# The second parity's value stores go from ScalarE's DMA queue to SyncE's

## The chip, the cores and the metric

One core of a Trainium2 chip runs the kernel. The metric is the device time of one execution in microseconds (us); before the change the median of three runs is 625.64 us. TensorE (PE) multiplies, VectorE (DVE) and ScalarE (ACT) copy, add and evaluate functions, GpSimd (POOL) issues accumulating transfers, and SyncE (SP) does nothing but issue transfers (DMAs). ScalarE can issue transfers too, and the change is about that. An engine runs its instructions in order: one that waits holds up all that stand behind it on that engine, computing ones included.

## The reference

For 2048 tokens x of width 512 the program computes g·a + (1 − g)·b, where g is a sigmoid gate of each token, a is attention with 32 heads of width 16 in which each token looks at itself and at 7 earlier tokens at distances 2, 4, ... 14, and b is a gated feed-forward net of width 1792.

```
q, k, v = split(x @ wqkv)                       # 32 heads of 16
idx = pos[:, None] - arange(8)[None, :] * 2     # 8 tokens, 2 apart
attn = softmax(where(idx >= 0, q . k[idx] * 16**-0.5, -1e9))
a = (sum over the 8 of attn * v[idx]) @ wo
b = (gelu(x @ w_gate) * (x @ w_up)) @ w_down
out = g * a + (1 - g) * b,   g = sigmoid(sum(x * gate_w))
```

## The kernel before, in words

**Parities.** The distances are even, so even and odd tokens never meet in the attention. The kernel does the even tokens first (`par` 0), then the odd ones (`par` 1), each as 8 tiles of 128 tokens, `jj` 0 to 7. The two halves run through the same stages: projections, then 14 feed-forward steps `f`.

**Projections.** `project` and `project_one` go through a parity's 8 tiles for a block `cb` of the weights `wqkv`: block 0 makes keys and queries of the first 16 heads, block 1 the values of both halves of the heads with the gate's column, block 2 keys and queries of the other 16 heads. Each product (L189, tile `acc` or `p` in PSUM) is made from numbers split in two parts, high and low, so it takes three matmuls for each of four slices of 128. Block 1 has two PSUM tiles for each `jj`, 16 in all, which take the four banks `acc0` to `acc3` in turn: a bank can be filled again only after its last tile was copied out.

**Taking a tile out.** `take` does that. ScalarE copies the PSUM tile into a staging tile in SBUF (L211; `hh` and `hl` in turn, six buffers of each; the last three of block 2 use `c`), a transfer stores it to memory in HBM (L215, `vs` for values, `ks` for keys; for keys there is a second one at L217 for the queries, `qs`), and for every other value tile ScalarE copies the gate's column (L219, tile `z`). A staging buffer can be written again only after the transfers that read it have landed. The attention reads `ks`, `qs`, `vs` back later, shifted by token: tiles `kq` (L270, L271, L267) and `v` (L270, L271).

**Around the values of the second parity.** At the same time SP loads what comes next: the weights of block 2 (`r`, L173, which ScalarE at L162 and VectorE at L87 split into `d`), feed-forward weights (`raw`, L461 and L463; `r`, L415; `g` from `ws`, L435), and the attention's `kq`. POOL adds into `g` (L440). VectorE runs the attention of the first parity (L286 to L337) and of the feed-forward (L488 to L495) in between.

**What sets the order.** The code is written as one stream; a scheduler that simulates a time line puts the instructions of each engine in order and adds the semaphore waits. Where one engine's queue changes, it may put other instructions in another order too. Transfers from SP and ACT share eight semaphores, `DMAHW0` to `DMAHW7`, which are given out in turn over both queues. A transfer waits, before it is issued, until the last transfer with its semaphore has landed, whichever engine issued that one. So ScalarE can be held by a store, and SP by a load of its own eight transfers ago.

**Which queue.** One line of `take` chooses (L214). Before, it sends keys and queries of the first parity and of the second head half to SP, and the rest to ACT: the second parity's keys and queries of block 0 (16 transfers), and all values (16 transfers in each parity).

Of the kernel before, what the change touches and what calls it, by code (L numbers as in the profile page):

```python
# [44 lines left out]
def tile_gated_mix(ctx: ExitStack, tc: tile.TileContext, xt, wqkv, wff, wo, out):  # L45
    nc = tc.nc
# [10 lines left out]
    def tl(tag, dt=F32):  # L57
        return pool.tile([P, COLS.get(tag, 512)], dt, name=tag, bufs=BUFS[tag])
# [146 lines left out]
    def rows(t, jj):  # L205
        return t.rearrange("c (p j) d -> j p c d", j=NP)[jj]

    def take(ps, par, jj, hh, vals, tag=None):
        st = tl(tag or next(stages))[:, :512]
        n = CU if vals else 512  # L210
        nc.scalar.activation(st[:, :n], ps[:, :n], AF.Copy)  # L211
        two = st.rearrange("p (a c d) -> p a c d", a=2, c=2)
        dst = VS[par, hh] if vals else KS[par, hh]
        queue = nc.sync if not vals and (hh or not par) else nc.scalar  # L214
        queue.dma_start(rows(dst[:, W:], jj), two[:, 0])  # L215
        if not vals:
            queue.dma_start(rows(QS[par, hh], jj), two[:, 1])  # L217
        elif not hh:
            nc.scalar.activation(z[:, par, jj:jj + 1], ps[:, CU:CU + 1], AF.Copy)  # L219

    def project(par, cb, bg=iter(())):
        for jj in range(NP):
            if cb == 1:
                for hh in range(2):

                    ps = bank(f"acc{(2 * jj + hh) % BT}")
                    qkv_mm(ps, par, jj, 1, range(KC), (CU, 0)[hh], (WQ, CU)[hh])
                    take(ps, par, jj, hh, True)
            else:
                ps = bank(next(names))  # L230
                qkv_mm(ps, par, jj, 0, range(KC))
                take(ps, par, jj, 0, False)
            next(bg, None)
            pull((2.7, 2.2)[par])
        done.add((par, cb))
        if cb == 1:
            en = pool.tile([P, 64], F32, name="en")[:, :NP]
            nc.scalar.activation(en, z[:, par], AF.Exp, scale=-1.0)
            nc.vector.tensor_scalar_add(en, en, 1.0)
            nc.vector.reciprocal(g[:, par], en)  # L240
            nc.vector.tensor_scalar(gc[:, par], g[:, par], -1.0, 1.0, op0=OP.mult, op1=OP.add)

    def project_one(par, jj):

        ps = bank(f"acc{jj % BT}")
        qkv_mm(ps, par, jj, 2, range(KC))
        take(ps, par, jj, 1, False, tag=None if jj < 5 else "c")
        pull((2.7, 2.2)[par])
        if jj == NP - 1:
            done.add((par, 2))  # L250
# [640 lines left out]
```

## Time and profile before

| what | value |
|---|---|
| median of three runs | 625.64 us (623.52 to 625.9) |
| the profiled execution, its own time | 623.92 us |
| its span in the trace | 622.1 us |
| TensorE busy | 606.0 us (97%) |
| TensorE weight loads | 505.5 us (81%) |
| VectorE busy | 514.1 us (83%) |
| ScalarE busy | 378.3 us (61%) |
| transfers issued by SP (q1) | 92.69 MB |
| transfers issued by ACT (q10) | 6.43 MB |

The span is the trace's own length, from which places in time are counted; the execution's time is 1.8 us longer. "Busy" leaves out the time in which an engine issues transfers or waits. In the chain of waits each piece is followed back to what released it; a row of the timeline gives start, length, engine, line and operation, and in brackets the idle time ahead of it with what ended that. `ACTq` and `SPq` are the instruction queues of ScalarE and SP: their DMA rows are issues, not the transfers. The second parity's values are made in the stretch from about 317 us to 344 us of the span.

### The profile page before, as it was taken

The numbers are of one execution on the slowest core, as the hardware profiler recorded it, in microseconds if no ns is written. First come the engines' busy times: TensorE is split into PE (matmuls) and PEld (weight loads), VectorE is DVE, ScalarE is ACT, GpSimd is POOL, SyncE is SP. The second block draws the span as 40 slices with busy tenths as digits, with TensorE's granted clock in tenths as the row PEclk, the third lists the DMA queues.
The fourth block names the chain that finished last, engine by engine and source line by source line (L and its number), as shares of the span: only waits on it lengthen the run. The fifth ranks groups of instructions, "written<-read, shape, count | busy, mean of one in ns | idle before, by whom it ended". The sixth has DMA issues, their size and how long they took to land.

```text
span 622.1 us, 8227 instructions
## 1 busy us (share of the span) xinstructions
PE 606.0 (97%) x2839; PEld 505.5 (81%) x2839; DVE 514.1 (83%) x598; ACT 378.3 (61%) x634; POOL 82.5 (13%) x110
## 2 busy tenths in 40 slices
PE   8999999999999999999996999999999999999997
PEld 7898877877888888888896887888888887888886
DVE  6949698969979797845985997999898979898881
ACT  6654456765776877764482337566766585685732
POOL 0141021111111111101100001111111011101200
PEclk9999999999999999999997999999999999999999
DMA  8399959796899988985478948886878597937624
GB/s 272 122 252 249 340 142 301 185 283 196 240 240 237 306 211 241 253 244 190 136 214 264 268 144 212 257 232 153 251 184 241 135 259 185 272 97 196 94 58 160
DMA packets 85591, 132.48 MB, mean 213 GB/s; under 512 B 8111, under 2 KB 52271, under 8 KB 85550
## 3 DMA queue, kind: packets, MB, share of 16 engines
q1 hardware_dynamic: 59678, 92.69, 45.2%
q0 software_dynamic: 12672, 32.84, 28.1%
q10 hardware_dynamic: 13200, 6.43, 3.5%
q8 instruction: 22, 0.36, 0.2%
q14 instruction: 19, 0.16, 0.1%
HBM read 67.18 MB, written 36.77 MB: 167 GB/s over the span
## 4 chain that ended last, share of the span: by engine, by line
PE 71%; DMA 13%; issue 7%; DVE 6%; ACT 2%; SPq 0%; POOL 0%; ACTq 0%; POOLq 0%; DVEq 0%
PE p L478 32%; PE acc L518 10%; PE acc L189 10%; PE p L518 10%; PE p L740 5%; DMA g<-raw 4%; DMA raw<-wff 4%; PE acc L740 2%; DMA vs<-hh 2%; PE p L189 2%; DMA c<-wqkv 1%; DMA d<-r 1%; DMA raw<-xt 1%; DVE prod L324 1%; DVE prod L286 1%
## 5 line engine op out<-in xcount | busy, mean ns | idle before, releaser
L478 PE MATMUL p<-S,g 128*128 128x512 f32 x672 | 166.4, 389 | 0.5 <-DVE c L488 0.5
L478 PEld LDWEIGHTS p<-S,g 128*128 128x128 f32 x672 | 126.0, 188 | 27.0 <-DVE c L488 0.9
L478 PE MATMUL p<-A,g 128*128 128x512 f32 x504 | 128.1, 391 | 3.9 <-DMA g<-raw 1.6
L478 PEld LDWEIGHTS p<-A,g 128*128 128x128 f32 x504 | 93.8, 188 | 26.3 <-DMA g<-raw 3.6
L286 DVE TENSOR_TENSOR prod<-kq 128x2048 f32<-128x2048 f32 x32 | 73.0, 2282 | 14.6 <-DMA kq<-kq 5.8
L440 POOL DMA_DIRECT2D g<-raw x42 | 36.4, 874 | 329.4 <-ACT g L439 202.5
L324 DVE TENSOR_TENSOR prod<-v,lg 128x2048 f32<-128x2048 f32 x32 | 73.0, 2280 | 6.3 <-DMA v<-vs 4.8
L289 DVE TENSOR_REDUCE lg<-prod 128x128 f32<-128x2048 f32 x32 | 73.0, 2282 | 0.3
L518 PE MATMUL p<-d,hh 128*128 128x512 f32 x224 | 68.7, 389 | 0.0
L518 PE MATMUL acc<-d,hh 128*128 128x512 f32 x224 | 60.5, 390 | 1.1 <-DMA d<-r 1.1
L444 ACT ACTIVATE g<-raw 128x1024 fp32r<-128x1024 f32 (+1 forms) x42 | 41.3, 988 | 18.8 <-PE p L478 18.8
L518 PEld LDWEIGHTS acc<-d,hh 128*128 128x128 f32 x224 | 42.0, 188 | 10.7 <-DMA d<-r 1.9
L518 PEld LDWEIGHTS p<-d,hh 128*128 128x128 f32 x224 | 42.0, 188 | 8.8
L439 ACT ACTIVATE g<-raw 128x1024 fp32r<-128x1024 f32 (+1 forms) x42 | 41.3, 983 | 10.5 <-DVE raw L421 9.7
L488 DVE TENSOR_TENSOR c<-p,s 128x512 f32<-128x512 f32 x56 | 38.1, 684 | 11.3 <-PE p L478 11.0
L492 DVE TENSOR_TENSOR c<-c 128x512 f32<-128x512 f32 x56 | 38.3, 685 | 10.7 <-ACT c L584 10.2
L483 ACT ACTIVATE s<-p 128x512 f32<-128x512 f32 x56 | 33.1, 593 | 17.3 <-PE p L478 17.1
L495 DVE TENSOR_TENSOR hl<-c,hh 128x512 fp32r<-128x512 f32 x56 | 38.2, 683 | 6.2 <-ACT hh L494 6.2
L518 PE MATMUL p<-d,hl 128*128 128x512 f32 x112 | 42.9, 389 | 0.0
L494 ACT ACTIVATE hh<-c 128x512 fp32r<-128x512 f32 x56 | 35.0, 625 | 11.6 <-DVE c L492 11.2
L531 ACT ACTIVATE rt<-p 128x512 f32<-128x512 f32 x48 | 28.0, 595 | 20.2 <-PE p L518 20.0
L328 DVE TENSOR_TENSOR prod<-prod 128x1024 f32<-128x1024 f32 x32 | 39.0, 1219 | 0.3
(145 smaller groups left out, 915.1 us busy)
## 6 DMA issues: line engine op xcount, KB each, us to landing
g<-raw POOLq DMA_DIRECT2D x28, 512.0 KB, 6.6
raw<-wff SPq DMA_DIRECT2D x42, 256.0 KB, 4.0
ws<-g SPq DMA_DIRECT2D x14, 768.0 KB, 6.1
g<-ws SPq DMA_DIRECT2D x14, 768.0 KB, 5.9
r<-wff SPq DMA_DIRECT2D x28, 256.0 KB, 4.4
d<-r POOLq DMA_DIRECT2D x28, 256.0 KB, 6.6
g<-raw POOLq DMA_DIRECT2D x14, 384.0 KB, 6.0
v<-vs SPq DMA_DIRECT2D x8, 512.0 KB, 7.4
```

Of the source, the lines that this page charges most:

```text
L189: LAST[:] = [nc.tensor.matmul(ps[:, :cn], a[:, t], w[:, c0:c0 + cn], start=(kc == 0 and n == 0), stop=(kc == KC - 1 and n == 2))]
L286: paced(nc.vector.tensor_tensor(prod, spans(k, jj), q[:, jj:jj + 2, None, :].to_broadcast([P, 2, W, UC]), op=OP.mult))
L289: nc.vector.tensor_reduce(two_of(lg, jj), prod.rearrange("p j w (h d) -> p (j w) h d", d=DH), axis=AX.X, op=OP.add)
L324: paced(nc.vector.tensor_tensor(prod.rearrange("p j w (h d) -> p (j w) h d", d=DH), spans(v, jj).rearrange("p j w (h d) -> p j w h d", d=D ...
L328: nc.vector.tensor_tensor(prod[:, :, :4], prod[:, :, :4], prod[:, :, 4:], op=OP.add)
L439: nc.scalar.activation(lo, raw, AF.Copy, scale=-1.0)
L444: ins = nc.scalar.activation(hi, raw, AF.Copy)
L478: LAST[:] = [nc.tensor.matmul(ps, w_, a_, start=(start and kc == 0 and n == 0), stop=(kc == 1 and n == 2), skip_group_check=True)]
L492: nc.vector.tensor_tensor(ge, ge, up, op=OP.mult)
L495: nc.vector.tensor_tensor(hl_, ge, hh_.bitcast(F32), op=OP.subtract)
L518: LAST[:] = [nc.tensor.matmul(pp, a[:, ts], w, start=(i == 0 and n == 0 and gr == 0), stop=(i == 1 and n == 2), skip_group_check=True)]
L740: LAST[:] = [nc.tensor.matmul(pa, a, b, start=(first and n == 0), stop=(last and n == 2), skip_group_check=True)]
```

## The change

One condition is written anew. Values of the second parity go to SP; every other store keeps its queue (keys and queries of the second parity's block 0 stay on ScalarE, as do the first parity's values).

```
-        queue = nc.sync if not vals and (hh or not par) else nc.scalar
+        queue = nc.sync if (vals if par else not vals) or hh and not vals else nc.scalar
```

So 16 transfers of 128 KB, with the waits that belong to them, leave ScalarE's stream and enter SP's. The scheduler's order is the same in both programs up to that place and differs behind it on all engines. Three places follow; in the names, numbers tell buffers apart, and in brackets stand the semaphores that an instruction waits for.

First, ScalarE's stream in the middle of the second parity's values. `hl_3188`, `hh_3168`, `hh_3205`, `hl_3224` are staging tiles, `vs10` and `vs11` the values in HBM, `d_3041` and `d_3046` the last two quarters of block 2's weights. Before:

```order
L215 DMA vs11_122<-hh_3125 128x2x128 [waits DMAHW4_49,Activation_49]
L553 ACTIVATE p_3374<-p_3367 128x512
L211 ACTIVATE hh_3168<-acc1_3155 128x256 [waits PE_49]
L215 DMA vs10_119<-hl_3151 128x2x128 [waits DMAHW6_49,Activation_49]
L211 ACTIVATE hh_3205<-acc3_3192 128x256 [waits PE_49]
L215 DMA vs10_119<-hl_3188 128x2x128 [waits DMAHW2_49,Activation_49]
L162 ACTIVATE d_3041<-r_3042 128x512 [waits DMAHW5_49]
L483 ACTIVATE s_3423<-p_3416 128x512 [waits DMASW7_49,PE_49]
L215 DMA vs11_122<-hh_3168 128x2x128 [waits DMAHW4_49,Activation_49]
L215 DMA vs11_122<-hh_3205 128x2x128 [waits Activation_49]
L211 ACTIVATE hl_3224<-acc0_3211 128x256 [waits PE_49]
L219 ACTIVATE z_132<-acc0_3211 128x1
```

and with the change:

```order
L439 ACTIVATE g1_3128<-raw_3053 128x1024 [waits DMAHW5_49,DMAHW4_49]
L444 ACTIVATE g1_3128<-raw_3053 128x1024
L211 ACTIVATE hl_3188<-acc2_3175 128x256 [waits DMAHW2_49,PE_49]
L219 ACTIVATE z_132<-acc2_3175 128x1
L483 ACTIVATE s_3423<-p_3416 128x512 [waits DMASW7_49,PE_49]
L211 ACTIVATE hh_3168<-acc1_3155 128x256 [waits PE_49]
L162 ACTIVATE d_3041<-r_3042 128x512 [waits DMAHW4_49]
L162 ACTIVATE d_3046<-r_3047 128x512 [waits DMAHW5_49,DMASW1_49]
L211 ACTIVATE hh_3205<-acc3_3192 128x256 [waits PE_49]
L211 ACTIVATE hl_3224<-acc0_3211 128x256 [waits PE_49]
L219 ACTIVATE z_132<-acc0_3211 128x1
```

The stores and their waits are gone. The two weight copies of L162 now stand together, ahead of the copy into `hh_3205`, and `L439`/`L444` stand later than before.

Second, SP's stream at the same place, from the last weights of block 2 on. Before:

```order
L461 DMA raw_3056<-ws11_748 128x512 [waits DMAHW2_49,DVE_49]
L463 DMA raw_3056<-wff 128x2x256 [waits DMAHW3_49]
L173 DMA r_3042<-wqkv 128x512 [waits DMAHW5_49,DVE_49]
L173 DMA r_3047<-wqkv 128x512 [waits DMAHW7_49,DVE_49]
L270 DMA kq_3320<-ks10_118 128x896 [waits DMAHW6_49,DMAHW1_49,DMAHW0_49]
L271 DMA kq_3320<-ks10_118 128x1024 [waits DMAHW1_49]
L267 DMA kq_3320<-qs10_120 128x1024 [waits DMAHW4_49,DMAHW3_49]
L461 DMA raw_3364<-ws21_950 128x512 [waits DMAHW6_49,DMASW2_49,Activation_49]
```

and with the change:

```order
L461 DMA raw_3056<-ws11_748 128x512 [waits DMAHW2_49,DVE_49]
L463 DMA raw_3056<-wff 128x2x256 [waits DMAHW3_49]
L173 DMA r_3042<-wqkv 128x512 [waits DMAHW4_49,DVE_49]
L173 DMA r_3047<-wqkv 128x512 [waits DMAHW5_49,DVE_49]
L215 DMA vs11_122<-hh_3125 128x2x128 [waits DMAHW6_49,Activation_49]
L215 DMA vs10_119<-hl_3151 128x2x128 [waits DMAHW7_49,Activation_49]
L270 DMA kq_3320<-ks10_118 128x896 [waits DMAHW0_49]
L215 DMA vs10_119<-hl_3188 128x2x128 [waits DMAHW1_49,Activation_49]
L271 DMA kq_3320<-ks10_118 128x1024 [waits DMAHW2_49]
L215 DMA vs11_122<-hh_3168 128x2x128 [waits DMAHW3_49,Activation_49]
L267 DMA kq_3320<-qs10_120 128x1024 [waits DMAHW4_49]
L215 DMA vs11_122<-hh_3205 128x2x128 [waits DMAHW5_49,Activation_49]
```

Stores now stand between the loads, and a load behind a store also waits until ScalarE has made the copy that this store sends.

Third, SP's stream just ahead of that, with the first value stores (`hl_3072`, `hl_3108`, `hh_3089`), with the change; before, the three `L215` rows are not there:

```order
L215 DMA vs10_119<-hl_3072 128x2x128 [waits DMAHW2_49,Activation_49]
L461 DMA raw_3053<-ws01_746 128x512 [waits DMAHW4_49,DVE_49]
L463 DMA raw_3053<-wff 128x2x256 [waits DMAHW5_49]
L215 DMA vs10_119<-hl_3108 128x2x128 [waits DMAHW7_49,Activation_49]
L215 DMA vs11_122<-hh_3089 128x2x128 [waits DMAHW1_49,Activation_49]
L461 DMA raw_3056<-ws11_748 128x512 [waits DMAHW2_49,DVE_49]
```

The load of `raw_3056` has the same semaphore as the store of `hl_3072`, five rows ahead, so it now waits for that store to land, and the weights `r_3042` and `r_3047` stand behind it.

## The prediction

> **What bounds the kernel now.** I read the page first, then the stretches of the projections, then the chain, the waits and the timelines of the worst stretch. Page:
>
> ```profile
> span 622.1 us, 8227 instructions
> ...
> PE 606.0 (97%) x2839; PEld 505.5 (81%) x2839; DVE 514.1 (83%) x598; ACT 378.3 (61%) x634; POOL 82.5 (13%) x110
> ```
>
> TensorE sets the time: 606.0 of 622.1 us. A change of queue can win only the 16.1 us in which it is idle and what its clock loses. Where these are, the stretches say (length; busy time and instructions of PE, weight loads, DVE, ACT, POOL; granted clock; DMA share; GB/s):
>
> ```profile
> 284.00:325.00 41.00, 41.00 (x229) 35.84 (x228) 33.02 (x47) 24.62 (x47) 5.26 (x9) 1.00 0.60 187
> 325.00:335.00 10.00, 5.62 (x47) 5.42 (x46) 5.44 (x6) 2.53 (x8) 0.00 (x0) 0.93 0.85 253
> 335.00:349.00 14.00, 13.20 (x72) 12.29 (x73) 11.33 (x15) 5.59 (x16) 0.87 (x1) 0.81 0.90 261
> 349.00:374.00 25.00, 25.00 (x112) 20.71 (x111) 23.86 (x17) 8.84 (x13) 0.00 (x0) 1.00 0.65 189
> 374.00:390.00 16.00, 14.91 (x67) 12.00 (x66) 12.46 (x16) 13.09 (x20) 2.59 (x3) 1.00 0.88 226
> 410.00:565.00 155.00, 154.32 (x681) 127.35 (x680) 141.84 (x148) 104.66 (x167) 17.50 (x21) 1.00 0.76 204
> ```
>
> The second and third stretch are the second parity's values: PE loses 4.4 and 0.8 us there, and of these stretches only there the clock falls (0.93, 0.81). Before and behind it PE is full or lacks about 1 us. In the chain (start, us, what):
>
> ```profile
> 323.62 10.67 DMA vs<-hh
> ...
> 335.58 0.17 ACT z L219
> 335.75 0.04 issue
> 335.80 13.53 PE acc L189 x72
> ```
>
> A store of 128 KB (`vs<-hh`) takes 10.67 us to land; ScalarE cannot issue the next store before that. Behind the issue stand the copies that empty the banks, and TensorE starts again 0.05 us after the gate's column is out. This is the program's order: the store of `hh_3168` waits for `DMAHW4`, which the store of `hh_3125` had. The waits there give the size:
>
> ```profile
> ACT hl L211 <- issue: 7.8, 1, 7.8
> DVE d L87 <- ACT d L162: 6.3, 1, 6.3
> ...
> PE acc L189 <- ACT z L219: 5.2, 1, 5.2
> ```
>
> One wait, 7.8 us on ScalarE, 6.3 on VectorE, 5.2 on TensorE.
>
> **What the change removes.** First, that wait. Second, the slow clock behind it, from TensorE's timeline:
>
> ```profile
> 326.14 0.88 PE L189 MATMUL acc<-g,rt 128*128 128x258 f32 x6
> ...
> 327.10 0.88 PE L189 MATMUL acc<-g,rt 128*128 128x256 f32 x6
> ...
> 329.03 0.88 PE L189 MATMUL acc<-g,rt 128*128 128x256 f32 x6
> ...
> 335.80 1.66 PE L189 MATMUL acc<-g,rt 128*128 128x258 f32 x6 [5.18 <-ACT z L219]
> ...
> 340.81 0.88 PE L189 MATMUL acc<-g,rt 128*128 128x258 f32 x6
> ...
> 342.26 0.88 PE L189 MATMUL acc<-g,rt 128*128 128x256 f32 x6
> ```
>
> (The first three rows serve further down.) Twelve matmuls, one tile, take 342.26 − 340.81 = 1.45 us at the full clock. The two tiles from 335.80 to 340.81 took 5.01 where 2.90 would do: 2.1 us lost. Stall and slow clock: 5.2 + 2.1 = **7.3 us**.
>
> Third, the issues themselves, and what the stores take to land:
>
> ```profile
> L215 ACTq DMA_DIRECT2D vs<-hl x8: 366/390/1058, 317.1 to 342.9; - x8
> L215 ACTq DMA_DIRECT2D vs<-hh x8: 366/366/482, 319.4 to 344.9; - x8
> DMA to landing us min/median/max: 1.8/4.1/10.7
> ```
>
> Sixteen at about 0.38 us are 6.1 us of ScalarE's stream. Without the wait they would be covered: ScalarE is busy 24.6 of 41 us in the stretch ahead. I count them as nothing; they enter through ScalarE's pace below.
>
> **What it adds on SP.** The same 6.1 us of issues, on a queue with room. It must not hold a load that somebody needs soon:
>
> ```profile
> 289.45 0.61 SPq L170 DMA_DIRECT2D c<-wqkv  x1
> 316.54 0.33 SPq L461 DMA_DIRECT2D raw<-ws  x1
> ...
> 320.14 0.33 SPq L461 DMA_DIRECT2D raw<-ws  x1
> ...
> 321.07 1.10 SPq L173 DMA_DIRECT2D r<-wqkv  x2
> 322.51 0.33 SPq L270 DMA_DIRECT2D kq<-ks  x1
> ...
> 334.74 0.32 SPq L461 DMA_DIRECT2D raw<-ws  x1
> ```
>
> SP issues nothing between 289.45 and 316.54. The urgent loads are the two `r<-wqkv`: ScalarE copies them (L162) now just ahead of the copy into `hh_3205`. In front of them come three value stores. The store of `hl_3072` goes out about 316.1 us, when its copy is done (315.65 + 0.37, below), and lands, at the median of 4.1, by 320.2; `raw_3056`, which waits for it, was issued at 320.14 anyway. So the `r` loads go out 0 to 0.5 us later than at 321.07 to 321.8. The rows of tile `r` in that stretch have landings of
>
> ```profile
> DMA to landing us min/median/max: 4.4/4.6/5.2
> ```
>
> so they are there by 325.5 to 327.5. The `kq` loads come about one store's landing later, 4.1 us (they stand behind the store of `hh_3125`), but VectorE starts on that `kq` only when the first parity's mixing is over; its timeline still has
>
> ```profile
> 344.69 2.25 DVE L324 TENSOR_TENSOR prod<-v,lg 128x2048 f32<-128x2048 f32 x1
> ```
>
> so even 7 us earlier there is room. `raw_3364` was held to 334.74 by the same kind of wait.
>
> **ScalarE's new pace.** Starting at `hh_3125` (now 319.78, some 0.4 earlier without the issue ahead of it, so 319.4), from its own rows: copy 0.39, L553 0.60, two issues for `ks` and `qs` 0.9, hl and z 0.53, table 1.28 and exp 0.63, L439 and L444 2.1, hl and z 0.52, L483 0.60 put the copy into `hh_3168` at about 327.0 and its end at 327.4. Rows are read start to start, so they overlap by some 0.1 us each and the sum is a little long. Quoted for the large ones:
>
> ```profile
> 315.65 0.37 ACT L211 ACTIVATE hl<-acc 128x256 f32<-128x256 f32 x1
> ...
> 319.78 0.39 ACT L211 ACTIVATE hh<-acc 128x256 f32<-128x256 f32 x1 [0.46 <-ACT hh L211]
> ...
> 322.26 1.28 ACT L304 ACT_TABLE_LOAD   x1
> ...
> 324.09 1.04 ACT L444 ACTIVATE g<-raw 128x1024 fp32r<-128x1024 f32 x1
> ...
> 326.39 0.65 ACT L162 ACTIVATE d<-r 128x512 fp32r<-128x512 f32 x1
> ```
>
> Then two L162 (1.2) and `hh_3205` by 329.0. TensorE wants those banks, by its rows above, at 326.1 (after `hl_3188` and its z, out at 326.3), 327.1 (after `hh_3168`, 327.4) and 329.0 (after `hh_3205`, 329.0). So it waits 0.2 to 0.5 us if the `r` loads land by 327.5, and as much more as they are late. Ends: nothing, and about 2 us if both come 2 us late. I take **0.8 us**, near the low end, since the landings vary by 0.8 only. In the stretch from 374 to 390 PE lacks 1.09 us and the clock stays at 1.00, so nothing is added for a slow clock.
>
> **Staging buffers.** A buffer comes back after twelve tiles, at 1.45 us each 17 us. The slowest of these stores took 10.67. So no copy waits for a buffer, with 6 us to spare; this cover goes if SP holds a store that long.
>
> **Behind it.** From 349 to 565 TensorE is full, so a gain made at 335 stays, if VectorE (141.84 of 155) keeps up. It loses the same gap, 6.3 us, so it falls back by 1 us at most. The scheduler's new order there I price at 0, ±1.5 us: the only gap is 16.0 − 14.91 = 1.1 us.
>
> **Sum.** 7.3 − 0.8 = 6.5 us. The profiled execution's 623.92 gives 617.4. It lies 1.7 us under the runs' median of 625.64 and near their lowest; I move up by half of that and predict **618.2 us**.
>
> **The rivals.** What speaks against the change is in the Trainium skill, "DMA: Bandwidth & Descriptors", section "Queues, rings and completion order": each DMA engine takes turns between the queue rows, packet by packet. By that, a store on ACT's row passes SP's loads and one on SP's row stands behind them. The trace disagrees for this store: on its own row it took 10.67 us while SP's loads ran. By the rule the sum would lose part of its gain in SP's row, which is rival A, at 621.5.
>
> A. *Late loads or stores, in part.* In SP's row three `kq` loads stand among the stores. If the `r` loads land at 330 to 331, or a store costs its buffer's 6 us of cover, TensorE waits 3 to 4 us in place of 0.8, with up to 1 us for the clock. For it: ScalarE now reaches L162 within 1 us of the expected landing. Against: 4.4 to 5.2 is a narrow spread. Net gain 2.3 to 4.3; 623.92 − 3.3, moved up by the same 0.8, is about 621.5.
>
> B. *The same wait in another place.* The change moves 2 MB but removes none, and the transfers' share is 0.85 to 0.90 there. If transfers and not the order of issues are the bound, ScalarE waits as long for `r` or for buffers. Against: TensorE, not transfers, was full again at 349 with 0.65. Then 624 to 625.
>
> C. *Slower.* The store of `hl_3072` is itself slow: every load behind `raw_3056` waits for it. Over all value and key stores the issue-to-landing times are
>
> ```profile
> DMA to landing us min/median/max: 1.8/3.9/12.9
> ```
>
> With 12.9, it lands at 329.0, the `r` loads go out at 330.5, land at 335.7, and the bank is free at 337.0 in place of 329.0: a gap of 8.0 us, and 2.1 for the clock, where 7.3 went: 623.92 + 2.8 = 626.7, more with another late bank. It decides if the `r` loads land after about 333. Against: SP's row is empty when that store goes out.
>
> D. *The change does nothing.* The order shows the sixteen stores gone from ScalarE; only the eight tiles of keys and queries of block 0 stay there. It can be left out.
>
> **Chances.** The forecast 0.62, its own range 615 to 621 (6.5 + 1.1 + 1 below the profiled time, and the lower gain on the median). A 0.17, B 0.13, C 0.08. Half a per cent, 3.1 us, is about what a measurement of this kernel can tell: faster means under 622.5, slower over 628.8. Faster: the forecast and most of A, 0.76; within: B, the rest of A and half of C, 0.18; slower: the other half, and a little for the new order, 0.06. The range, 614.5 to 623.5, holds the forecast and A and leaves out B and C, 2 in 10.
>
> **What would show it.** In the changed profile: no wait of ScalarE on an issue at L215 near 327; the stretch from 325 to 349 with PE full at a clock of 1.00; no 5 us on "PE acc <- ACT z"; VectorE's wait at L87 under 1 us. Against it: a wait "ACT d L162 <- DMA r" of several us (A or C), "ACT L211 <- DMA vs" (buffers), or gaps of TensorE of more than 2 us behind 349.

## The result, and the profile after

| | before | after |
|---|---|---|
| median time | 625.77 us (623.52 to 626.91, 4 runs) | 616.54 us (614.47 to 616.72, 4 runs) |
| profiled execution, its own time | 623.92 us | 614.47 us |
| its span | 622.1 us | 612.5 us |

The ratio after to before is 0.9849, 95% interval 0.9815 to 0.9884: faster by 1.5%. Predicted were 618.2 us, range 614.5 to 623.5.

The page of the changed kernel:

```profile
span 612.5 us, 8244 instructions
...
PE 602.3 (98%) x2839; PEld 503.6 (82%) x2839; DVE 514.1 (84%) x598; ACT 376.4 (61%) x633; POOL 82.5 (13%) x110
```

The same 2839 matmuls take 3.7 us less busy time and stand in a span that is 9.6 us shorter. To see where, I cut both traces at two places that both programs have: the first feed-forward matmuls among the second parity's values (`p<-A,g`), and the first matmul of block 2 (`acc<-d,A`). Between them lies the same work: 156 matmuls start there, and the rows count those at the edges too, 158 here and up to 159 further down. The stretch between the two (length; busy time and instructions of PE, weight loads, DVE, ACT, POOL; granted clock; DMA share; GB/s), before:

```profile
316.18:343.69 27.51, 22.33 (x158) 21.61 (x157) 17.41 (x24) 14.00 (x36) 0.88 (x1) 0.88 0.88 256
```

and after:

```profile
316.40:336.46 20.06, 20.06 (x158) 19.55 (x157) 18.46 (x25) 14.20 (x38) 0.89 (x1) 1.00 1.00 302
```

That is 7.45 us: 27.51 − 22.33 = 5.18 us in which TensorE stood, and 22.33 − 20.06 = 2.27 us of slow clock. Behind the second cut to the end of the span, before needs 622.1 − 343.69 = 278.41 us and after 612.5 − 336.46 = 276.04: another 2.37 us. Ahead of the first cut after is 0.22 us later. 7.45 + 2.37 − 0.22 = 9.60, the whole difference of the spans.

The chain of waits of the changed kernel, start, length and what:

```profile
320.82 1.39 PE p L478 x6
322.21 19.89 PE acc L189 x144
342.09 1.36 PE p L478 x6
```

Where the chain went through a store (`vs<-hh`, 10.67 us) and ScalarE before, there now is nothing but TensorE. ScalarE's timeline at the place of the old wait:

```profile
325.51 0.40 ACT L211 ACTIVATE hh<-acc 128x256 f32<-128x256 f32 x1
326.36 1.32 ACT L162 ACTIVATE d<-r 128x512 fp32r<-128x512 f32 x2 [0.46 <-DMA r<-wqkv]
327.58 0.37 ACT L211 ACTIVATE hh<-acc 128x256 f32<-128x256 f32 x1
...
328.86 0.39 ACT L211 ACTIVATE hh<-acc 128x256 f32<-128x256 f32 x1 [0.57 <-PE acc L189]
```

The copies into `hh_3168` (325.51) and `hh_3205` (327.58) have the two weight copies of L162 between them. The one wait left there is 0.46 us for a load. At 328.86 ScalarE waits for TensorE, and TensorE has no wait in the whole stretch. SP's timeline:

```profile
321.53 0.89 SPq L173 DMA_DIRECT2D r<-wqkv  x2
322.51 0.38 SPq L215 DMA_DIRECT2D vs<-hh  x1
...
323.46 0.74 SPq L270 DMA_DIRECT2D kq<-ks  x1
...
327.48 1.26 SPq L267 DMA_DIRECT2D kq<-qs  x1
```

The last `kq` load goes out at 327.48, 3.1 us later than before. The value stores stand between, and some are held themselves (issues of up to 1.26 us). On SP no copy stands behind them.

### The profile page after: what moved, and what is told of

Its sections match the earlier page's. It is cut to its first block, busy times and chain, and to the rows that moved or that the text cites. A ratio compares the mean times of both kernels' runs of the same rounds, so it can differ in the third digit from the quotient of the medians.

```text
span 612.5 us, 8244 instructions
## 1 busy us (share of the span) xinstructions
PE 602.3 (98%) x2839; PEld 503.6 (82%) x2839; DVE 514.1 (84%) x598; ACT 376.4 (61%) x633; POOL 82.5 (13%) x110
## 4 chain that ended last, share of the span: by engine, by line
PE 84%; DMA 6%; issue 5%; DVE 2%; ACT 1%; SPq 0%; POOL 0%; DVEq 0%; ACTq 0%; POOLq 0%
PE p L478 38%; PE acc L189 13%; PE acc L518 11%; PE p L518 11%; PE p L740 5%; PE p L189 3%; PE acc L740 2%; DMA v<-vs 1%; DMA raw<-wff 1%; DMA c<-wqkv 1%; DMA d<-r 1%; DMA raw<-xt 1%; DVE prod L324 1%; DMA ws<-raw 1%; ACT s L526 1%
## 5 line engine op out<-in xcount | busy, mean ns | idle before, releaser
L444 ACT ACTIVATE g<-raw 128x1024 fp32r<-128x1024 f32 (+1 forms) x42 | 41.3, 988 | 13.1 <-PE p L478 12.8
L439 ACT ACTIVATE g<-raw 128x1024 fp32r<-128x1024 f32 (+1 forms) x42 | 41.3, 983 | 10.3 <-DVE raw L421 10.0
```

Of the source, the lines that this page charges most:

```text
L439: nc.scalar.activation(lo, raw, AF.Copy, scale=-1.0)
L444: ins = nc.scalar.activation(hi, raw, AF.Copy)
```

## The experiments

What I held for the cause: a store that ScalarE may not issue until another transfer, the last one with the same semaphore, has landed; that other one is slow beside SP's `kq` loads; and the copies that free TensorE's banks stand behind the store that waits. The rivals: that sixteen issues were simply too much for ScalarE; that a store is late wherever it goes; that the scheduler's new order, not the stores, made the gain; and that SP's order of loads decides. Each kernel is compared with runs of the kernel before on its own chip (medians 625.81 and 625.80 us). All are cut at the same two places, as above; the last four columns are of the one profiled execution of each:

| kernel | median, us | ratio, 95% interval | to first cut | between cuts | behind | span |
|---|---|---|---|---|---|---|
| before | 625.8 | 1 | 316.18 | 27.51 | 278.41 | 622.1 |
| changed | 616.54 | 0.9849 [0.9815, 0.9884] | 316.40 | 20.06 | 276.04 | 612.5 |
| middle stores on SP | 618.73 | 0.9899 [0.9867, 0.9931] | 318.12 | 22.80 | 275.98 | 616.9 |
| the others on SP | 614.72 | 0.984 [0.9796, 0.9883] | 316.37 | 20.54 | 275.59 | 612.5 |
| all sixteen on POOL | 615.38 | 0.9851 [0.9808, 0.9893] | 317.99 | 20.06 | 276.75 | 614.8 |
| `kq` loads later only | 618.15 | 0.9886 [0.9836, 0.9936] | 318.24 | 20.06 | 279.20 | 617.5 |
| two small stores more | 626.34 | 1.0017 [0.999, 1.0043] | 316.87 | 28.98 | 278.65 | 624.5 |
| every store on SP | 621.62 | 0.9932 [0.9896, 0.9968] | 317.38 | 20.06 | 281.86 | 619.3 |
| changed, `kq` later | 615.64 | 0.9834 [0.9798, 0.987] | 316.58 | 20.07 | 276.25 | 612.9 |
| changed, again | 616.22 | 0.9848 [0.9818, 0.9879] | 317.02 | 20.07 | 276.11 | 613.2 |

The way to the first cut varies by some 2 us, and between two executions of the changed kernel by 0.6; the two columns behind it are what an edit is read from.

### The middle stores alone

Only the value stores of three tiles (`jj` 1 to 3, both halves, six stores; the store that waited before is one of them) go to SP.

```
-        queue = nc.sync if not vals and (hh or not par) else nc.scalar
+        queue = nc.sync if not vals and (hh or not par) or (vals and par and 0 < jj < 4) else nc.scalar
```

> Six of the sixteen second-parity value stores go to SP (tiles jj 1 to 3, the ones around the wait of 7.8 us); the other ten stay on ScalarE. Theory (one wait of ScalarE, at the store of hh_3168, that held for a landing): the six are enough; no issue of ScalarE waits more than 2 us between 318 and 345 us, the 5.2 us gap of TensorE and its slow clock are gone, and the span falls by 6.5 to 9.5 us, to about 613 to 616. Rival R (the gain is ScalarE's relief from sixteen issues of 0.38 us): 6/16 of the 9.6 us, so about 618.5. Rival S (later stores on ScalarE wait in its place, behind the kq loads): a gap of 3 us or more comes back a few tiles later, span 618 to 622.

Measured: 22.80 us between the cuts. The span, 616.9 us, is above what the theory gave and below both rivals, but the way to the first cut is 1.9 us longer here than before, so the span alone tells none of them apart.

```profile
318.12:340.92 22.80, 21.28 (x160) 20.10 (x159) 18.59 (x25) 12.92 (x34) 0.88 (x1) 1.00 0.94 282
```

It holds two matmuls more than the changed kernel's, feed-forward ones that the scheduler put here (six take 1.39 us in the chain above, so two 0.46). So 22.80 − 20.06 − 0.46 = 2.3 us of the 7.45 are still lost. ScalarE's and TensorE's waits from 316 to 350:

```profile
ACT d L162 <- DMA r<-wqkv: 3.6, 2, 2.5
...
ACT hl L211 <- DMA vs<-hh: 3.2, 2, 2.6
...
PE acc L189 <- ACT z L219: 1.4, 1, 1.4
```

The long wait is gone, and two smaller kinds come in its place. The stores that stayed on ScalarE wait for a store (2.6 us); in the chain of waits that is one on SP's queue, which took 6.52 us. And the `r` loads come late: in this order they stand behind the first `kq` load, ahead of which SP issued nothing for 4 us:

```profile
324.24 0.32 SPq L270 DMA_DIRECT2D kq<-ks  x1
...
325.13 0.86 SPq L173 DMA_DIRECT2D r<-wqkv  x2
```

So the order of SP's loads can cost something, as a rival said, and a store on SP can hold one on ScalarE. TensorE's 1.4 us end with the second wait; how the 2.3 us divide between the loads and the stores that stayed, the trace doesn't separate.

### The other ten, with the middle six left on ScalarE

```
+        queue = nc.sync if not vals and (hh or not par) or (vals and par and not 0 < jj < 4) else nc.scalar
```

> The reverse: the ten other value stores of the second parity go to SP, the six of tiles jj 1 to 3 stay on ScalarE. Theory: stores that stand beside the loads of kq are still on ScalarE, so one of them (hh_3168 or hh_3205) still holds ScalarE for a landing of 5 to 11 us; TensorE has a gap of 2 to 6 us near 328 to 336 and the span is 617 to 622. Rival R: 10/16 of the gain, about 616, without a gap of more than 1 us.

Measured: I had expected a wait of 5 to 11 us to remain, since the store that waited is still on ScalarE, and a span of 617 to 622. No such wait remained, and the span is 612.5; the rival with its 10/16 of the gain missed too. The stretch:

```profile
316.37:336.91 20.54, 20.54 (x161) 19.94 (x160) 19.15 (x26) 14.06 (x38) 0.89 (x1) 1.00 0.98 293
```

TensorE never stands. The 0.48 us above 20.06 are two feed-forward matmuls again. Yet the four stores issued from 324 to 329, three of them on ScalarE, are as slow as before:

```profile
DMA to landing us min/median/max: 7.0/9.4/10.4
```

So a slow store alone does no harm, and it isn't the place of this store that makes the wait. What differs is who holds its semaphore: in this order the store of `hh_3168` follows the store of `hl_3151`, which went out at 321.62, ahead of the first `kq` load at 323.21, and landed within 3.1 us.

### All sixteen on POOL's queue

```
+        queue = nc.gpsimd if vals and par else nc.sync if not vals and (hh or not par) else nc.scalar
```

> All sixteen go to GpSimd's queue. Theory: that they leave ScalarE is what counts, whatever takes them; the gap of 5.2 us is gone and the span is 612.5 to 617. Rival Q (SP's row is the better one, since there the stores stand in line with the loads): on a third row the stores take 10 us and more beside the loads; but as nobody waits for them on ScalarE, a loss could come through staging buffers alone (a wait of L211 on a landing), which then shows as more than 2 us. Rival: GpSimd's accumulations into g (L440) come late behind the stores and TensorE waits for g, 1 to 4 us.

Measured: 615.38 us, like the changed kernel, with the same stretch.

```profile
317.99:338.05 20.06, 20.06 (x159) 19.55 (x158) 18.31 (x25) 13.55 (x36) 11.44 (x16) 1.00 0.97 309
```

SP has no part in the gain. It is enough that the stores leave the engine that frees TensorE's banks. They are not faster there (the stores of L215 from 316 to 346 took 6.0 us at the median, 9.2 at most), but ScalarE waits 1.0 us at most for one and TensorE not at all.

### The stores as before, the `kq` loads later

This leaves all sixteen stores on ScalarE. `paced` ties an instruction to the one that the scheduler placed last; with it the three `kq` loads of the second parity stand behind `raw_3364` and two loads of `r`. Only SP's order differs from the kernel before; that of the other engines is the same.

```
-        load_slots(k, KS[par, hh][c])
-        nc.sync.dma_start(q, QS[par, hh][c]...)
+        load_slots(k, KS[par, hh][c], paced if par and not u else lambda x: x)
+        (paced if par and not u else lambda x: x)(nc.sync.dma_start(q, QS[par, hh][c]...))
...
-    def load_slots(t, src):
-        nc.sync.dma_start(...)
+    def load_slots(t, src, wait=lambda x: x):
+        wait(nc.sync.dma_start(...))
```

> Stores stay on ScalarE as before. Only SP's order changes: the three loads of kq for the second parity stand behind the loads of raw_3364 and of two r, which wait for a buffer; all other engines keep the order of the kernel before. Theory (the store of hh_3125 lands late because SP's loads of kq fill the transfer engines, and ScalarE's next store waits for it): without them it lands in 2 to 5 us, ScalarE waits under 2 us, TensorE's gap is under 1.5 us and its clock stays full; the later gaps of 1.4 us near 385 and 1.0 us near 520, in the order of before, stay. Span 614 to 617, 1 to 3 us behind the changed kernel. Rival R (relief of issues): no gain, 622. Rival N (the scheduler's new order behind the stores makes the gain): no gain, 622.

Measured: the stretch is as short as in the changed kernel, with every store still on ScalarE. (The span is half a microsecond above what was expected; the way to the first cut is 2 us longer here than before.)

```profile
318.24:338.30 20.06, 20.06 (x159) 19.54 (x158) 16.80 (x22) 13.95 (x36) 0.89 (x1) 1.00 0.96 275
```

This refutes that sixteen issues were too much for ScalarE, and that a new order was needed for these 7.45 us. The stores show why. In the kernel before, the one issued between 322 and 324, that of `hh_3125`, took

```profile
DMA to landing us min/median/max: 10.7/10.7/10.7
```

and here the two issued between 326 and 328, at the same place in ScalarE's order, took

```profile
326.07 0.37 ACTq L215 DMA_DIRECT2D vs<-hh  x1
326.59 1.50 ACTq L215 DMA_DIRECT2D vs<-hl  x1
...
339.01 0.37 ACTq L215 DMA_DIRECT2D vs<-hl  x1
```

```profile
DMA to landing us min/median/max: 5.5/5.5/5.6
```

The `kq` loads now go out at 335.93 to 338.02, and the store issued behind them, at 339.01 (the last row of the timeline above), is the slow one:

```profile
DMA to landing us min/median/max: 10.1/10.1/10.1
```

So the stores around the old place are faster without the `kq` loads, and the slow one stands behind their new place, where SP's load of `g` (768 KB, at 338.60) is out too. No copy waits for it there. The order of SP's loads does decide, then, but as a part of this cause: it sets when the store lands whose semaphore ScalarE needs.

Behind the second cut this kernel is as long as before (279.20 and 278.41). TensorE's timeline and the chain name the longest gap there:

```profile
381.50 1.42 PE L478 MATMUL p<-A,g 128*128 128x512 f32 x5 [1.76 <-DMA g<-raw]
```

```profile
370.56 10.89 DMA g<-raw
```

The same gap is in the kernel before (1.09 us up to 386.23, behind a transfer of 10.22 us). In the changed kernel TensorE is full at that place:

```profile
366.00:380.00 14.00, 14.00 (x63) 11.60 (x62) 11.46 (x15) 12.53 (x20) 2.59 (x3) 1.00 0.94 238
```

So 7.45 us are the wait, and the 2.4 us behind come and go with the scheduler's order.

### Two small stores more

The stores as before; two transfers of 16 bytes follow the store of `hh_3125` on ScalarE. They only take two semaphores out of the turn; `EXTRA` is small tensors in HBM.

```
-        queue.dma_start(rows(dst[:, W:], jj), two[:, 0])
+        queue.dma_start(rows(dst[:, W:], jj), two[:, 0]), [nc.scalar.dma_start(EXTRA[i], st[:1, :4]) for i in range(2) if vals and par and hh and jj == 1]
```

> The stores as in the kernel before, and two transfers of 16 bytes more on ScalarE, right behind the store of `hh_3125`. They take two of the eight semaphores in turn, so the one which that store holds (`DMAHW4`) is now wanted by the store of `hl_3188`, ahead of the store of `hh_3168`, which follows one of the tiny ones. Semaphore theory: ScalarE waits at the store of `hl_3188`, 6 to 9 us until the store of `hh_3125` has landed, with the copy into `hh_3205` behind it; at the store of `hh_3168` it waits less than 1 us. TensorE stands 4 to 6 us and then has its slow clock: span 619 to 624. Rival (the store of `hh_3168` waits for its own reasons, such as a full row of ScalarE): the wait of 7 to 8 us stays at the store of `hh_3168`.

Measured: ScalarE's timeline, with the issues.

```profile
324.31 0.37 ACTq L215 DMA_DIRECT2D vs<-hh  x1
...
327.80 0.36 ACT L211 ACTIVATE hh<-acc 128x256 f32<-128x256 f32 x1
334.25 0.39 ACTq L215 DMA_DIRECT2D vs<-hl  x1
334.68 0.38 ACT L211 ACTIVATE hh<-acc 128x256 f32<-128x256 f32 x1 [6.52 <-DMA vs<-hh]
334.76 0.40 ACTq L215 DMA_DIRECT2D vs<-hh  x1
```

As the semaphores said: the store of `hl_3188`, which now has the semaphore of the store of `hh_3125` (issued at 324.31), waits until 334.25, and the one of `hh_3168`, which waited before, follows 0.5 us later without a wait of its own. TensorE stands for as long as before:

```profile
335.12 1.65 PE L189 MATMUL acc<-g,rt 128*128 128x256 f32 x6 [5.21 <-ACT hh L211]
```

The stretch is 1.5 us longer than before (28.98 to 27.51), the time the same within the interval; the span of 624.5 lies half a microsecond above what was expected. A rival cause in the store of `hh_3168` itself is out.

### Every store on SP

```
-        queue = nc.sync if not vals and (hh or not par) else nc.scalar
+        queue = nc.sync
```

> All stores of all projections on SP, those of the first parity's values and of the second parity's keys and queries of block 0 too. If leaving ScalarE is all that counts: no wait of ScalarE above 2 us in the values of the second parity, span 611 to 615, the same as the changed kernel within 0.5%. If the changed kernel's gain hangs on its own order of loads: gaps of TensorE elsewhere, span 616 to 622.

Measured: 621.62 us. The stretch is 20.06 us again, so the gain of the changed kernel is there; but behind it 281.86 us, 5.8 more than in the changed kernel, so it lands on the second of the two expectations. Most of that is one place, where a transfer to `d` comes late; in the chain of waits the loads of `r` ahead of it took 8.27 us. TensorE's timeline, and the clock in the stretch behind:

```profile
397.33 2.01 PE L518 MATMUL acc<-d,hh 128*128 128x512 f32 x4 [2.98 <-DMA d<-r]
```

```profile
397.33:400.00 2.67, 2.67 (x7) 2.10 (x8) 2.44 (x2) 0.00 (x0) 0.00 (x0) 0.52 0.49 141
```

The stall of 2.98 us and the slow clock, 2.67 × 0.48 = 1.3 us and another 0.4 us from 400 to 404 (4 us at 0.90), are 4.7 of the 5.8. More of the same edit is worth less: what it wins in one place, the scheduler's order loses in another.

### The changed kernel with the `kq` loads later, and the changed kernel again

The edit to the `kq` loads of above, made in the changed kernel, and the changed kernel as it is beside it.

> The changed kernel, and its three `kq` loads of the second parity go out later, behind stores of the values; TensorE, VectorE, ScalarE and POOL keep their order word for word. If nothing but the wait behind the `kq` loads was at work, there is nothing left to win: span 611 to 615, within 0.3% of the changed kernel. If the `kq` loads still cost it something (ScalarE's 0.46 us at L162), up to 0.5 us less; if VectorE needs `kq` early, 1 to 3 us more.

> The changed kernel once more, to stand beside the three others of this call. Expected as before: span 612.5 to 615, time 614.5 to 617; no wait of ScalarE on an issue above 1 us in the values of the second parity.

Measured: 615.64 and 616.22 us, ratios 0.9834 and 0.9848 with intervals that overlap almost wholly; between the cuts 20.07 us in both. With the stores off ScalarE, the `kq` loads have nothing left to hold. No version that I ran is faster than the changed kernel beyond the noise: the lowest median, 614.72 us with ten stores on SP, has an interval of 0.9796 to 0.9883 beside 0.9815 to 0.9884.

## Why the prediction was right

The time was in the range, and the forecast's mechanism is what happened. By its steps:

**What it removes, 7.3 us.** Right: 7.45 us, of which 5.18 the stall and 2.27 the clock, where 5.2 and 2.1 were forecast. One sentence there is loose: ScalarE could issue the next two stores, at 324.14 and 325.44; the third, with the same semaphore, was held.

**The issues, counted as nothing.** Right, and shown: with all sixteen still on ScalarE and the `kq` loads held, TensorE is full over the whole stretch.

**ScalarE's new pace, 0.8 us.** Too much; it was nothing. The copy into `hh_3168` was forecast to end at 327.4 and ended at 325.91 (325.51 + 0.40): the sum of ScalarE's steps was 1.5 us too long. It counts two issues for `ks` and `qs`, 0.9 us, behind the copy into `hh_3125`; in the trace they stand ahead of it, at 318.05 and 318.53 (before: 317.54 and 318.02). The rest is mostly the overlap of rows read start to start, which I had called only a little. The `r` loads went out at 321.53 (forecast 321.07 to 321.8) and held L162 until 326.36 (forecast 325.5 to 327.5), so the loads were sized well. TensorE waited 0, inside the ends given.

**Staging buffers, nothing.** Right. The stores of L215 from 316 to 346 took, from issue to landing, in the kernel before

```profile
DMA to landing us min/median/max: 1.8/3.9/10.7
```

and in the changed one

```profile
DMA to landing us min/median/max: 2.3/5.1/7.6
```

against 17 us until a buffer is wanted again. In SP's row the median store is slower and the slowest one faster. Beside rival A stood a rule of the Trainium skill ("DMA: Bandwidth & Descriptors", section "Queues, rings and completion order"): each DMA engine takes turns between the queue rows, packet by packet. I wrote that the trace disagrees, and I had read it wrongly. The rows do take turns (last section); what doesn't follow is that a store on ScalarE's row passes SP's loads, since its packets are a seventh of theirs and its first one came after 4 us.

**Behind it, 0 ± 1.5 us.** The step that failed. It was 2.37 us. The forecast called the 1.1 us at 386.23 the only gap, though a row that it quotes has 155.00 − 154.32 = 0.68 us more, and it didn't ask whether the new order keeps them. Both are missing after; they are 1.77 of the 2.37 us, and the rest is too finely spread to be placed. The window of the trace from 401 to 556 of the changed kernel, which answers to 410 to 565 before, has no idle time where 0.68 stood:

```profile
401.00:556.00 155.00, 155.00 (x686) 128.28 (x685) 143.38 (x147) 104.44 (x168) 17.49 (x21) 1.00 0.75 204
```

**From the profiled time to the median.** The working's 617.4 should have been 623.92 − 9.6 = 614.3, and the profiled execution took 614.47. I had moved 0.8 us up because the profiled execution before was a quick one; the one after was quicker still against its median (2.1 us below). The misses of the sum (0.8 and 2.4) made the forecast too high, this one made it too low, so 618.2 came out only 1.7 too high. That they offset each other is luck; the mechanism is not.

**The rivals.** A and B (the wait in another place) did not come true in this kernel; A's mechanism is real: where only the middle stores were moved, late `r` loads held ScalarE for up to 2.5 us. C hung on the store of `hl_3072`: issued at 316.5 on SP, it landed within 2.4 us, and the load behind it went out at 320.63. D was out from the start.

Left open: why the scheduler's orders differ by up to 6 us behind the second cut (275.59 to 281.86). I showed which gaps are there, not which of its choices makes them.

## What to carry to other kernels

An engine that frees the buffers of the bottleneck should not issue transfers whose semaphore another engine's traffic can hold: what it pays isn't the issue of 0.4 us but the wait in front of it, here 7.8 us once, with everything queued behind. Before moving stores, read which earlier transfer has the same semaphore and what is on the wire at that time; to hold three loads back, or to move the stores to SP's or to POOL's queue, bought the same 7.45 us. And after any such edit look at the gaps behind it in the new order, since these moved the time by another 2 to 6 us.

## What was not expected of the hardware

**A store on a row of its own can wait 4 us for its first packet, and then takes turns with larger ones.** The DMA view of the kernel before, when the store of `hh_3125` (issued at 323.62) and two more were out (queue: packets, MB, share of 16 engines; q1 is SP's row, q0 POOL's, q10 ScalarE's), from 324 to 328 us

```profile
q1 hardware_dynamic: 320, 0.77, 73.4%
q0 software_dynamic: 51, 0.21, 26.1%
q10 hardware_dynamic: 2, 0.00, 0.1%
```

and from 328 to 332:

```profile
q1 hardware_dynamic: 227, 0.84, 53.4%
q0 software_dynamic: 93, 0.32, 39.7%
q10 hardware_dynamic: 216, 0.11, 9.1%
```

ScalarE's row had 384 KB waiting. For 4 us it moved next to nothing; after that it moved as many packets as SP's row, but of 0.5 KB each (0.11 MB in 216) beside 3.7 KB (0.84 MB in 227). The cleanest stretch is in the kernel with the other ten stores on SP, from 330 to 333:

```profile
q0 software_dynamic: 98, 0.40, 66.9%
q1 hardware_dynamic: 97, 0.36, 32.9%
q10 hardware_dynamic: 96, 0.05, 5.6%
```

The Trainium skill ("DMA: Bandwidth & Descriptors", section "Queues, rings and completion order") lets the rows take turns, packet by packet. These rows agree with it, as far as the profile's packets are those that the Trainium skill means: the turns are equal in packets, so the bytes go by the size of a packet, and a store of small packets is slow beside loads of large ones. In the kernel with the `kq` loads later ScalarE's row also moved next to nothing at first (20 packets from 327 to 329.5, the first store issued at 326.07), but then SP's row was empty, and it moved 0.57 MB from 329.5 to 331.5. So by these rows most of the difference between 10.7 and 5.5 us lies in the turns and not in the start.

The same section of the Trainium skill says that a transfer's semaphore rises only after every earlier write of its DMA engine, across queues. That would hold a store behind the loads too; but by 332, 8.4 us after the first issue, the row had moved 218 of the some 770 packets of its three stores, so the bytes themselves were late. Why the first packet comes so late, no run tells.

**The clock forgives short gaps.** TensorE's stalls of 1.4 us (middle stores, row of the stretch above) and of 1.76 us (`kq` loads later) left the granted clock at 1.00. Behind the second the window reads

```profile
381.50:386.00 4.50, 4.50 (x20) 3.71 (x21) 3.82 (x4) 2.14 (x4) 0.00 (x0) 1.00 1.11 296
```

The stall of 2.98 us (every store on SP) was followed by 2.67 us at 0.52, and that of 5.18 us before by 5.01 us for work of 2.90. So what a gap costs beyond itself began, in these runs, somewhere between 1.8 and 3 us; no stall between the two was seen.
